# The first steps of an attention and feed-forward kernel, listed in another order

## The chip, the cores and the metric

The kernel runs on one NeuronCore of a Trainium2 chip. The metric is device time in microseconds (us) of one execution. An execution is also recorded by the hardware profiler; its span runs from the first to the last instruction of the program. The core's engines are PE (TensorE, matmuls and transposes into PSUM), DVE (VectorE), ACT (ScalarE), POOL (GpSimd) and SP (SyncE, which here only issues DMAs). Each takes its own instructions strictly in the order in which they were written.

## The reference

```python
# attention in chunks of 64 tokens: B=8, H=8, S=576, D=64
scores = scale * np.matmul(q_c, k_c.transpose(0, 1, 2, 4, 3))
scores = scores - np.max(scores, axis=-1, keepdims=True)
attn = np.exp(scores)
attn = attn / (np.sum(attn, axis=-1, keepdims=True) + 1e-09)
out = np.matmul(attn, v_c)
# the heads side by side give x of 4608 tokens x 512; then, with d_ff = 1024:
h = x @ w_in
e = np.exp(h - h_max)
sm = e / (np.sum(e, axis=-1, keepdims=True) + 1e-09)
solu = h * sm
ln = (solu - mu) / np.sqrt(var + 1e-06) * g_ln
return (ln @ w_out).astype(np.float32)
```

q, k and v are float32; w_in (512 x 1024) and w_out (1024 x 512) come as 64-bit floats, 4 MB each; g_ln has 1024 values.

## The kernel before

The 4608 tokens are 36 tiles of 128. A tile holds two chunks of 64 tokens with all 8 heads. Its way is: q and k (256 KB each) are loaded and turned, scores (PE), softmax (DVE, ACT, POOL or DVE), the weights turned, values (PE), the product with w_in into `ph` (PE), its softmax, sum and mean (DVE, ACT), z turned and split, the product with w_out (PE), and the store.

The products are made in pieces. A weight is split into a high and a low part (`wi_h`, `wi_l`, `wo_h`, `wo_l`), and the product of a tile with w_in is 24 matmuls of 128x128 by 128x512. Tiles 0 and 1 are an exception (FM = 2): they take the unsplit float32 weight `w_a` and the unsplit `x_f`, 8 matmuls that show as 16 in the profile.

The weights come in eight units: units 0 to 3 are 128 rows of w_in, 4 to 7 are 256 rows of w_out, 1 MB each as raw 64-bit words (`w_raw`). A unit passes through steps that other words of the list name: P loads it; c scales it (DVE or POOL by CL_DVE, then ACT); C shifts it and adds the low bits (two instructions of DVE); t makes the high part (ACT); D makes the low part (POOL for the halves in SUB_POOL, else DVE). With C done, `w_a` of the unit can be multiplied.

Up to tile 5 the order is written out by hand: START (lines 19 to 33) is a list of words, and lines 815 to 823 run them one after the other. A word as `N:2:1` is a step with its numbers; a word that stands several times continues its step each time from where it stopped. The words that matter here:

- n:i loads q and k of tile i in their natural layout (`nat`, or `nat_z` for tiles 2 and 3). N:i:0 and N:i:1 turn q and k of it: first four transposes on PE into a PSUM bank `po`, the second time the copy to `qT` or `kT` (DVE for those in NV_DVE, else ACT). There are two `po` banks, which N, T, z and F share.
- S:i scores; A:i maximum and subtraction (DVE), the second time the exponential (ACT); B:i sum and reciprocal (DVE), then the scaling of `e` (POOL for tiles in NORM_POOL, else DVE); T:i transposes `e` on PE and copies it to `attn_t`.
- v:i loads v; V:i values, then `x_f`, or `x_h` and `x_l`.
- M:i the product with w_in. M:0 goes on in four parts, one for each unit of w_in. X:i maximum, exponential; Y:i the product of `ph` and its exponential, which leaves z and frees `ph`; there is one `ph` buffer, so M:i+1 waits for Y:i. F is a third of a tile's product with w_out.
- W:x multiplies the identity by itself, with no use of the result. g loads g_ln, G turns it.

Behind START a loop makes tiles 5 to 35 in a fixed pattern, with tile i's product with w_in beside tile i-1's and i-2's product with w_out. SP issues nearly all loads into one queue, and a DMA's issue waits until the DMA eight places earlier has landed, or until a buffer is free.

Of the kernel before, what the change touches and what calls it, by code (L numbers as in the profile page):

```python
# [12 lines left out]
AF = mybir.ActivationFunctionType  # L13
# [3 lines left out]


START = """
W:41 W:42 n:0 n:1 N:0:1 N:0:0 N:0:0 N:0:1 N:1:0 n:2 S:0 N:2:1 N:1:0 A:0 A:0 P0 P1 P:2 N:1:1 B:0  # L20
P:1 c:0 c:2 N:1:1 W:43 c:0 N:2:0 S:1 W:44 W:45 W:46 N:2:1 N:2:0 n:3 c:2 C:0 A:1 A:1 C:0 B:0 c:1
B:1 S:2 T:0 N:3:0 T:0 W:47 g W:4 c:1 N:3:0 A:2 v:0 C:2 N:3:1 P:3 G P:4 t:0 V:0 N:3:1 n:4 C:1 B:1
G V:0 A:2 S:3 C:1 C:2 T:1 B:2 B:2 c:3 c:3 M:0 t:2 M:0 A:3 C:3 T:1 M:0 v:1 A:3 C:3 c:4 B:3 M:0
N:4:1 X:0 t:1 N:4:0 c:4 n:5 N:4:1 T:2 v:2 B:3 N:4:0 n:6 X:0 V:1 C:4 v:3 P:5 P:6 D:1:0 T:2 Y:0
S:4 T:3 C:4 N:5:0 V:1 A:4 t:3 A:4 P:7 T:3 D:1:1 M:1 t:4 N:5:1 D:3:1 B:4 D:2:1 N:5:0 D:0:1 D:2:0
D:0:0 Y:0 N:5:1 V:2 N:6:1 D:3:0 v:4 D:4:0 N:6:0 c:5 B:4 D:4:1 V:2 S:5 X:1 n:7 N:6:1 X:1 V:2 Y:1
z:0:1 N:6:0 V:3 z:0:1 c:5 R:0 A:5 z:0:0 C:5 A:5 z:0:0 V:3 C:5 M:2 z:0:1 T:4 c:6 B:5 z:0:0 V:3
Q:2 S:6 t:5 c:6 N:7:0 T:4 X:2 C:6 V:4 q:8 v:5 N:7:0 B:5 n:8 D:5:1 c:7 D:5:0 T:5 X:2 Y:2 C:6 T:5
F c:7 Y:2 t:6 C:7 N:7:1 C:7 N:7:1 D:6:1 D:6:0 M:3 F t:7 D:7:0 A:6 V:4 N:8:0 V:4 D:7:1 R:2 q:8
Y:1 N:8:0 V:5 S:7 X:3 Z:2 X:3 N:8:1 Y:3 A:7 N:8:1 A:6 q:8 q:8 F z:1:0 z:1:0 R:1 A:7 B:6 v:6  # L30
z:1:0 M:4 V:5 B:7 B:6 Y:3 U:6 o:0 B:7 Z:3 z:1:1 U:7 z:1:1 v:7 X:4 o:0 X:4 F z:1:1 Y:4 R:3 F K:9
F o:1 Y:4 o:1 V:5 R:4
"""


# [23 lines left out]
def chunk_attention_then_solu_ffn(  # L59
# [35 lines left out]
    MS = nc.gpsimd
# [29 lines left out]
    g_sb = const.tile([P, NFC], F32, name="g_sb")  # L125
    g_row = const.tile([NFC, P], F32, name="g_row")
# [10 lines left out]
    HALF = FF // 2  # L137
    raw_words = 2 if w_in.dtype != F32 else 1
# [28 lines left out]
    def unit_scale(x):  # L167
# [15 lines left out]
    def unit_round(x):  # L183
# [55 lines left out]
    QT, KT, V, QS, KS = {}, {}, {}, {}, {}  # L239
# [98 lines left out]
    def turn_natural(i, x):  # L338
# [25 lines left out]
    def attn(i, part):  # L364
        return (sx, sy)[i % 2 if order.on else part][:, :, part]
# [46 lines left out]
    def softmax_b(i):  # L412
# [15 lines left out]
    def attn_transpose(i):  # L428
# [148 lines left out]
    def solu_b(i):  # L577
# [162 lines left out]
    def load_first():  # L740
        load_pair(0)
        sync.dma_start(*early[0])
# [57 lines left out]
    def product():  # L800
# [150 lines left out]
```

## Time and profile before

| | |
|---|---|
| median of 3 runs | 476.33 us (475.26 to 476.84) |
| the profiled execution | 477.21 us, of which its span is 475.3 us |
| PE busy over the span | 461.9 us |
| DVE, ACT, POOL busy | 368.8, 249.9, 160.2 us |
| mean granted clock of PE | 0.993 |

The profiled execution took 0.88 us more than the median, and 1.9 us of it lie outside the span. A busy share of 97% on PE says that the span is nearly PE's work from end to end. In the 40 slices of the page only the first two and the last have PE below nine tenths; a slice is 11.9 us.

### The profile page before, as it was taken

What the parts mean: (1) busy time and instruction counts of PE and PEld (TensorE: products, weight loads), DVE (VectorE), ACT (ScalarE), POOL (GpSimd) and SP (SyncE); (2) the same over time, 40 slices, a digit from 0 to 9 for tenths busy, and PEclk for the clock granted to TensorE, in tenths of its full rate; (3) what the DMA queues carried; (4) which work ended last, traced back from release to release, by engine and by line L of the source; (5) the groups of instructions that cost most, each with busy time, mean ns of one, the idle gap of its engine ahead of it and who ended that gap; (6) DMA issues with size and microseconds to landing.
All of it is one profiled execution on the core that took longest, in us unless ns stands there. A gap on an engine that the chain in (4) does not pass through costs nothing.

```text
span 475.3 us, 10986 instructions
## 1 busy us (share of the span) xinstructions
PE 461.9 (97%) x4193; PEld 378.3 (80%) x4193; DVE 368.8 (78%) x511; ACT 249.9 (53%) x402; POOL 160.2 (34%) x305
## 2 busy tenths in 40 slices
PE   6699999999999999999999999999999999999996
PEld 5555888888888888888888888888888888888886
DVE  2799988798888787878788878797979797945430
ACT  2565985546464645454545555555555555554551
POOL 0338556350505050505050505032515141413300
PEclk9799999999999999999999999999999999999999
DMA  9999877878787877697348596948644435333211
GB/s 225 302 248 325 135 134 154 197 181 161 173 164 174 157 179 143 154 168 172 84 125 167 140 188 147 181 123 182 152 111 110 113 85 140 97 103 103 75 44 46
DMA packets 192996, 72.05 MB, mean 152 GB/s; under 512 B 177128, under 2 KB 177648, under 8 KB 192560
## 3 DMA queue, kind: packets, MB, share of 16 engines
q1 hardware_dynamic: 186528, 58.63, 55.4%
q0 software_dynamic: 6272, 12.60, 10.1%
q8 instruction: 33, 0.54, 0.5%
q14 instruction: 19, 0.16, 0.1%
q10 hardware_dynamic: 144, 0.13, 0.1%
HBM read 36.70 MB, written 9.44 MB: 97 GB/s over the span
## 4 chain that ended last, share of the span: by engine, by line
PE 94%; DMA 2%; SPq 2%; DVE 1%; issue 0%; DVEq 0%
PE po L50 44%; PE ph L50 42%; PE sx L50 5%; PE sy L50 4%; DMA nat_z<-in_q_dram 2%; SPq L50 2%; DVE w_a L50 0%; DVE z L50 0%; DVE h_nmax L50 0%; DVE qT L50 0%; DVE o_sb L50 0%; DVEq L50 0%
## 5 line engine op out<-in xcount | busy, mean ns | idle before, releaser
L50 PE MATMUL po<-wo_l,z_h 128*128 128x512 f32 x280 | 110.8, 396 | 0.0
L50 ACT ACTIVATE z<-ph,h_nmax 128x1024 f32<-128x1024 f32 x36 | 40.2, 1117 | 131.6 <-DVE h_nmax L50 131.5
L50 PE MATMUL po<-wo_h,z_h 128*128 128x512 f32 x280 | 109.3, 390 | 0.0
L50 PE MATMUL po<-wo_h,z_l 128*128 128x512 f32 x280 | 109.2, 390 | 0.0
L50 PE MATMUL ph<-wi_l,x_h 128*128 128x512 f32 x272 | 106.1, 390 | 0.0
L50 PE MATMUL ph<-wi_h,x_h 128*128 128x512 f32 x272 | 105.8, 389 | 0.0
L50 POOL TENSOR_TENSOR u<-ssq,eps 128x1 f32<-128x1 f32 x36 | 6.8, 189 | 225.6 <-ACT sq L50 225.6
L50 POOL DMA_DIRECT2D z_t<-z_b x136 | 67.7, 505 | 16.6 <-DVE z_b L50 10.5
L50 PE MATMUL ph<-wi_h,x_l 128*128 128x512 f32 x272 | 72.7, 389 | 0.0
L50 DVE TENSOR_REDUCE h_nmax<-ph 128x1 f32<-128x1024 f32 x36 | 44.0, 1221 | 34.8 <-PE ph L50 34.8
L50 PEld LDWEIGHTS po<-wo_l,z_h 128*128 128x128 f32 x280 | 52.5, 188 | 11.4
L50 PEld LDWEIGHTS po<-wo_h,z_l 128*128 128x128 f32 x280 | 52.6, 188 | 11.0
L50 PEld LDWEIGHTS po<-wo_h,z_h 128*128 128x128 f32 x280 | 52.6, 188 | 10.4
L50 PEld LDWEIGHTS ph<-wi_l,x_h 128*128 128x128 f32 x272 | 51.1, 188 | 10.7 <-issue 0.2
L50 PEld LDWEIGHTS ph<-wi_h,x_l 128*128 128x128 f32 x272 | 51.0, 188 | 10.6
L50 PEld LDWEIGHTS ph<-wi_h,x_h 128*128 128x128 f32 x272 | 51.1, 188 | 10.5
L50 DVE TENSOR_TENSOR z_l<-z_t,z_h 128x1024 fp32r<-128x1024 f32 (+1 forms) x35 | 40.7, 1164 | 21.0 <-ACT z_h L50 21.0
L50 DVE SCALAR_TENSOR_TENSOR z<-ph,z 128x1024 f32<-128x1024 f32 x36 | 44.0, 1224 | 13.8 <-ACT z L50 13.7
L50 ACT ACTIVATE z<-z,z_sum 128x1024 f32<-128x1024 f32 x34 | 39.2, 1153 | 21.4 <-DVE z L50 20.3
L50 DVE STREAM_TRANSPOSE z_b<-z 128x1024 f32<-128x1024 f32 x33 | 39.9, 1209 | 6.6 <-ACT z L50 3.1
L50 ACT ACTIVATE o_sb<-po,r 128x512 f32<-128x512 f32 (+1 forms) x36 | 24.3, 675 | 28.5 <-POOL r L50 20.8
L50 ACT ACTIVATE sq<-z 128x1024 bf16<-128x1024 f32 x36 | 37.6, 1043 | 2.5 <-POOL z L50 2.5
(88 smaller groups left out, 621.8 us busy)
## 6 DMA issues: line engine op xcount, KB each, us to landing
out_dram<-o_sb SPq DMA_DIRECT2D x35, 256.0 KB, 2.5
z_t<-z_b SPq DMA_DIRECT2D x128, 64.0 KB, 2.9
z_t<-z_b POOLq DMA_DIRECT2D x128, 64.0 KB, 2.8
q_st<-in_q_dram SPq DMA_DIRECT2D x96, 72.0 KB, 3.2
k_st<-in_k_dram SPq DMA_DIRECT2D x96, 72.0 KB, 2.9
v_sb<-in_v_dram SPq DMA_DIRECT2D x27, 256.0 KB, 4.3
w_raw<-in_moe_w_out_dram SPq DMA_DIRECT2D x4, 1024.0 KB, 7.2
attn_t<-a_b POOLq DMA_DIRECT2D x60, 64.0 KB, 3.6
```

The lines of the kernel that those rows point to most:

```text
L50: ins = make(*args, **kwargs)
```

## The change

START is written anew, the lists that assign steps to engines change with it, and g_ln is loaded by ACT's queue. Every step of the old list is in the new one (the loads of tiles 0 to 8, eight W, the eight units, the products of tiles 0 to 4). The first words:

```diff
-W:41 W:42 n:0 n:1 N:0:1 N:0:0 N:0:0 N:0:1 N:1:0 n:2 S:0 N:2:1 N:1:0 A:0 A:0 P0 P1 P:2 N:1:1 B:0
-P:1 c:0 c:2 N:1:1 W:43 c:0 N:2:0 S:1 W:44 W:45 W:46 N:2:1 N:2:0 n:3 c:2 C:0 A:1 A:1 C:0 B:0 c:1
...
+n:1 n:0 P0 P1 P:1 P:2 n:2 W:41 W:44 W:4 W:43 N:1:0 N:1:0 W:42 v:0 c:0 N:0:1 N:0:1 c:0 N:0:0
+N:0:0 N:1:1 S:0 A:0 A:0 n:3 B:0 N:1:1 C:0 W:45 c:2 S:1 B:0 T:0 T:0 A:1 C:0 c:2 N:2:0 N:2:0
...
-    NV_DVE = ((0, 1), (1, 0), (2, 1), (4, 0), (6, 1), (9, 1),)
-    MEAN_POOL = (3, 4,)
-    CL_DVE = (0, 3, 4,)
-    TV_DVE = (3,)
-    SUB_POOL = ((0, 0), (0, 1), (1, 0), (1, 1), (2, 0), (2, 1), (3, 0), (3, 1), (7, 0), (7, 1),)
-    NORM_POOL = (0, 1, 2, 3, 4, 5, 6, 7,)
+    NV_DVE = ((0, 0), (2, 0), (5, 1), (8, 0), (9, 1))
+    MEAN_POOL = (0, 3, 4)
+    CL_DVE = (2, 3, 7)
+    TV_DVE = ()
+    GM_ACT = ()
+    SUB_POOL = ((0, 0), (0, 1), (1, 0), (1, 1), (2, 0), (2, 1), (3, 0), (3, 1), (5, 0), (5, 1), (6, 0))
+    NORM_POOL = (0, 1, 5, 6)
     SH_POOL = ()
+    HALF_IN = (3,)
...
-            sync.dma_start(dst, src)
+            cut = HALF * raw_words if x in HALF_IN else 2 * HALF * raw_words
+            if x >= NCC:
+                sync.dma_start(dst, src)
+            else:
+                for n in range(0, 2 * HALF * raw_words, cut):
+                    sync.dma_start(dst[:, n:n + cut], src[:, n:n + cut])
...
-        sync.dma_start(g_row, g_ln.rearrange("(a p) -> a p", p=P))
+        nc.scalar.dma_start(g_row, g_ln.rearrange("(a p) -> a p", p=P))
```

GM_ACT is empty, so the lines that ask for it change nothing.

On SP, at the start of the program, the loads stood so before (`nat` is tile 0, then 1; `nat_z` tile 2, then 3; `w_raw` from w_in units 0, 2, 1 and 3):

```order
L50 DMA nat<-in_k_dram 128x8x64
L50 DMA nat_z<-in_q_dram 128x8x64
L50 DMA nat_z<-in_k_dram 128x8x64
L50 DMA w_raw<-in_moe_w_in_dram 128x1024 x2
L50 DMA w_raw<-in_moe_w_in_dram 128x2048 x2
L50 DMA nat_z<-in_q_dram 128x8x64
L50 DMA nat_z<-in_k_dram 128x8x64
L50 DMA g_row<-in_moe_g_ln_dram 8x128
L50 DMA v_sb<-in_v_dram 128x4x64
L50 DMA v_sb<-in_v_dram 64x4x64 x2
L50 DMA w_raw<-in_moe_w_in_dram 128x2048
```

and stand so now (`nat` is tile 1, then 0; the first three units are 0, 1 and 2, the last two halves are unit 3):

```order
L51 DMA nat<-in_k_dram 128x8x64
L51 DMA w_raw<-in_moe_w_in_dram 128x1024 x2
L51 DMA w_raw<-in_moe_w_in_dram 128x2048 x2
L51 DMA nat_z<-in_q_dram 128x8x64
L51 DMA nat_z<-in_k_dram 128x8x64
L51 DMA v_sb<-in_v_dram 128x4x64
L51 DMA v_sb<-in_v_dram 64x4x64 x2
L51 DMA nat_z<-in_q_dram 128x8x64
L51 DMA nat_z<-in_k_dram 128x8x64
L51 DMA w_raw<-in_moe_w_in_dram 128x1024 x2
```

Four loads of q and k precede the weights instead of six, tile 2 comes behind unit 2, and v of tile 0 ahead of tile 3; up to unit 3 the same loads are made, without g.

On ACT the first instructions before (`qT`, `kT` are copies out of PSUM, `e_99` the exponential of tile 0, `w_a` the scaling of a unit):

```order
L50 ACT_TABLE_LOAD
L50 COPY qT<-po 128x512
L50 ACTIVATE e_99<-e_99 128x4x128
L50 COPY kT<-po 128x512
L50 ACTIVATE w_a<-w_a 128x1024
L50 COPY qT<-po 128x512
```

and now:

```order
L761 DMA g_row<-in_moe_g_ln_dram 8x128
L51 ACT_TABLE_LOAD
L51 COPY qT<-po 128x512
L51 COPY kT<-po 128x512
L51 ACTIVATE w_a<-w_a 128x1024
L51 ACTIVATE e_99<-e_99 128x4x128
L51 COPY kT<-po 128x512
L51 COPY attn_t<-po 128x8x2x32
```

Unit 0's scaling now stands ahead of tile 0's exponential and of the copy of tile 1's k, which the scores of tile 1 read.

On PE, the product of tile 0 (`ph<-w_a,x_f`) and what stands before it was:

```order
L50 MATMUL sy<-attn_t,v_sb 64x64 x16
L50 MATMUL sx<-kT,qT 64x64 x16
L50 MATMUL po<-ident,e_100 128x128 x4
L50 MATMUL ph<-w_a,x_f 128x512 x8
L50 MATMUL po<-ident,nat 128x128 x8
```

and is now:

```order
L51 MATMUL sy_98<-attn_t_95,v_sb_138 64x64 x16
L51 MATMUL ph_119<-ident_79 128x128 x4
L51 MATMUL sx_97<-kT_226,qT_225 64x64 x16
L51 MATMUL ph_303<-w_a_142,x_f_264 128x512 x2
L51 MATMUL po_308<-ident_79,nat_z_184 128x128 x4
L51 MATMUL po_313<-ident_79,nat_z_184 128x128 x4
L51 MATMUL ph_303<-w_a_233,x_f_264 128x512 x2
L51 MATMUL po_334<-ident_79,nat_96 128x128 x4
L51 MATMUL ph_303<-w_a_195,x_f_264 128x512 x2
L51 MATMUL po_352<-ident_79,nat_96 128x128 x4
L51 MATMUL ph_303<-w_a_327,x_f_264 128x512 x2
```

The product was one block behind the turning of tile 3; now its four parts (units 0, 1, 2, 3) lie around the turning of tile 3 and of tile 4.

## Rows read from the trace of the kernel before

**Rows 1.** Parts 1 and 2 of the page: PE, and its clock in tenths.
```profile
PE 461.9 (97%) x4193; PEld 378.3 (80%) x4193; DVE 368.8 (78%) x511; ACT 249.9 (53%) x402; POOL 160.2 (34%) x305
...
PEclk9799999999999999999999999999999999999999
```

**Rows 2.** Windows: stretch, its length, busy time by engine (instructions), clock, DMA.
```profile
14.70:18.90 4.20, 1.26 (x36) 1.01 (x36) 3.57 (x5) 2.73 (x4) 2.13 (x3) 1.00 1.11 322
18.90:25.70 6.80, 5.68 (x82) 5.25 (x81) 5.47 (x10) 4.33 (x7) 2.45 (x2) 0.50 0.85 267
...
34.00:49.90 15.90, 14.62 (x212) 9.19 (x210) 15.52 (x19) 10.75 (x18) 13.91 (x10) 1.00 1.06 289
...
50.00:60.00 10.00, 10.00 (x108) 8.24 (x109) 9.61 (x14) 8.83 (x16) 5.02 (x5) 1.00 0.69 120
```

**Rows 3.** The chain that ended last: start, length, engine and line.
```profile
26.39 7.00 PE ph L50 x16
...
35.23 1.75 DVE w_a L50
...
38.27 7.10 PE ph L50 x16
...
49.88 5.67 PE ph L50 x24
```

**Rows 4.** Timeline of PE: start, length, operation, count, idle before and its releaser.
```profile
1.42 2.07 PE L50 MATMUL ph<-ident 128*128 128x128 f32 x8 [1.42 <-POOL e L393]
5.30 3.02 PE L50 MATMUL po<-ident,nat 128*128 128x128 f32 x12 [1.80 <-DMA nat<-in_k_dram]
...
10.04 0.63 PE L50 MATMUL po<-ident,nat_z 128*128 128x128 f32 x4 [0.93 <-DMA nat_z<-in_k_dram]
...
13.09 1.60 PE L50 MATMUL ph<-ident 128*128 128x128 f32 x12
17.64 0.69 PE L50 MATMUL sx<-kT,qT 64*64 64x64 f32 x32 [2.95 <-DVE e L50]
...
20.04 1.09 PE L50 MATMUL po<-ident,nat_z 128*128 128x128 f32 x4 [1.12 <-DMA nat_z<-in_q_dram]
...
23.82 1.13 PE L50 MATMUL sy<-attn_t,v_sb 64*64 64x64 f32 x32
...
35.14 0.69 PE L50 MATMUL sy<-attn_t,v_sb 64*64 64x64 f32 x32
```

**Rows 5.** Timeline of SP: its issues of DMAs, start and length.
```profile
8.77 0.89 SPq L50 DMA_DIRECT2D nat_z<-in_q_dram  x1
9.71 5.12 SPq L50 DMA_DIRECT2D nat_z<-in_k_dram  x1
14.87 2.76 SPq L50 DMA_DIRECT2D g_row<-in_moe_g_ln_dram  x1
```

**Rows 6.** Timeline of POOL, 16 to 20 us.
```profile
16.07 1.09 POOL L50 TENSOR_SCALAR w_a<-w_raw 128x1024 f32<-128x1024 f32 x1 [14.63 <-DMA w_raw<-in_moe_w_in_dram]
17.14 1.04 POOL L50 TENSOR_TENSOR e<-e,s_rinv 128x512 f32<-128x512 f32 x1
18.88 1.42 POOL L50 TENSOR_SCALAR w_a<-w_raw 128x1024 f32<-128x1024 f32 x1 [0.71 <-DMA w_raw<-in_moe_w_in_dram]
```

**Rows 7.** Timeline of DVE, steps of units and a copy.
```profile
13.59 0.69 DVE L50 TENSOR_SCALAR w_a<-w_raw 128x1024 f32<-128x1024 f32 x1 [1.27 <-DMA w_raw<-in_moe_w_in_dram]
14.20 0.68 DVE L50 COPY kT<-po 128x512 f32<-128x512 f32 x1
...
29.98 1.35 DVE L50 SCALAR_TENSOR_TENSOR w_a<-w_raw,w_a 128x1024 uint16<-128x1024 uint32 x1
```

**Rows 8.** Timeline of ACT, 10 to 15 us.
```profile
11.26 0.57 ACT L50 COPY kT<-po 128x512 f32<-128x512 f32 x1
...
14.32 1.06 ACT L50 ACTIVATE w_a<-w_a 128x1024 f32<-128x1024 f32 x1 [2.49 <-DVE w_a L50]
```

**Rows 9.** DMA issues within 20.1 to 20.6 us: unit 3, count, size, us to landing.
```profile
w_raw<-in_moe_w_in_dram SPq DMA_DIRECT2D x1, 1024.0 KB, 5.1
```

More of the change, by code (lines that the diff above doesn't have):

```diff
@@ L19 @@
 START = """
-W:41 W:42 n:0 n:1 N:0:1 N:0:0 N:0:0 N:0:1 N:1:0 n:2 S:0 N:2:1 N:1:0 A:0 A:0 P0 P1 P:2 N:1:1 B:0
-P:1 c:0 c:2 N:1:1 W:43 c:0 N:2:0 S:1 W:44 W:45 W:46 N:2:1 N:2:0 n:3 c:2 C:0 A:1 A:1 C:0 B:0 c:1
[L22 to L32, printed above, removed]
+n:1 n:0 P0 P1 P:1 P:2 n:2 W:41 W:44 W:4 W:43 N:1:0 N:1:0 W:42 v:0 c:0 N:0:1 N:0:1 c:0 N:0:0
+N:0:0 N:1:1 S:0 A:0 A:0 n:3 B:0 N:1:1 C:0 W:45 c:2 S:1 B:0 T:0 T:0 A:1 C:0 c:2 N:2:0 N:2:0
+c:1 c:1 A:1 C:2 N:2:1 V:0 W:47 N:2:1 g C:1 V:0 P:3 n:4 W:46 S:2 B:1 C:1 A:2 v:1 M:0
+N:3:0 N:3:1 A:2 C:2 n:5 N:3:0 P:5 N:3:1 B:1 c:3 M:0 c:3 N:4:0 N:4:0 M:0 B:2 P:4 t:0 C:3 D:0:1
+C:3 N:4:1 t:1 N:4:1 t:3 M:0 D:3:0 D:1:1 n:6 T:1 D:3:1 B:2 S:3 T:1 X:0 T:2 N:5:0 X:0 A:3 T:2
+V:1 V:1 S:4 N:5:0 N:5:1 D:1:0 A:3 Y:0 A:4 M:1 N:5:1 A:4 c:5 B:3 B:3 c:5 c:4 t:2 v:2 c:4
+N:6:1 P:6 T:3 C:5 N:6:1 n:7 B:4 B:4 C:5 V:2 X:1 G T:3 C:4 T:4 D:0:0 G X:1 S:5 Y:1
+T:4 V:2 Y:0 z:0:1 v:4 v:3 D:2:0 V:2 A:5 t:5 D:2:1 z:0:1 z:0:0 z:0:0 z:0:0 P:7 M:2 c:6 A:5 C:4
+B:5 N:6:0 R:0 t:4 D:4:0 v:5 z:0:1 X:2 c:6 V:3 C:6 N:6:0 S:6 V:3 n:8 V:3 X:2 N:7:0 N:7:1 N:7:0
+Y:2 Y:2 B:5 C:6 c:7 V:4 D:4:1 T:5 V:4 t:6 D:5:0 N:7:1 Y:1 V:4 D:6:0 D:6:1 Z:2 A:6 D:5:1 T:5
+M:3 c:7 z:1:0 C:7 v:6 F Q:2 R:2 X:3 C:7 X:3 F S:7 z:1:0 t:7 Y:3 D:7:0 A:6 D:7:1 Y:3
+z:1:0 A:7 R:1 q:8 V:5 V:5 F o:0 q:8 q:8 z:1:1 z:1:1 M:4 q:8 N:8:1 A:7 B:7 v:7 z:1:1 B:6
+B:6 R:3 F F X:4 Z:3 X:4 Y:4 Y:4 B:7 N:8:1 U:6 V:5 U:7 R:4 F o:1 o:1 o:0 K:9
+N:8:0 N:8:0
 """
@@ L209, in unit_high @@
                 g = g_sb[:, 2 * m + y:2 * m + y + 1]
-                act.activation(top[:, y], a[:, y], AF.Copy, scale=g)
+                act.activation(
+                    a[:, y] if x in GM_ACT else top[:, y], a[:, y], AF.Copy, scale=g
+                )
+            if x in GM_ACT:
+                act.copy(top, a)
         tops[x] = top
@@ L221, in unit_rest @@
             low = wo_l[:, 2 * m + y, :]
-            g = g_sb[:, 2 * m + y:2 * m + y + 1]
+            if x not in GM_ACT:
+                g = g_sb[:, 2 * m + y:2 * m + y + 1]
         of, part = a[:, y], top[:, y].bitcast(F32)
```

## The prediction

> **What bounds the kernel now.** I read the page first, then windows, then the chain of waits, then the engines' timelines of the first 50 us. The page gives PE 461.9 us of 475.3 [rows 1], so at most 13.4 us can be won, and some 3.5 of them are the last store. The windows say where: from 50 us on PE is busy 10.00 of 10.00, before that 14.62 of 15.90 and less [rows 2]. The chain agrees: from the product at 49.88, the first with a split weight (tile 2, M:2), it is PE alone [rows 3]. The reader is to see the idle times in PE's timeline: 1.42, 1.80, 0.93, 2.95 and 1.12 us [rows 4], with 1.28 between 34 and 49.9 [rows 2], together 9.5. A second loss is the clock. From 18.9 to 25.7 us it is granted at 0.50 (1.2 of 2.4 GHz), after a stretch in which PE worked 1.26 of 4.20 us [rows 2]; 5.68 us of work there would take half, so 2.8 are lost. It is low at the start too, where the page's row says full [rows 1]: twelve transposes take 3.02 us there, twelve like matmuls at 13.09 take 1.60 [rows 4]. So I measure the change by when M:2 begins, how much of PE's work is done by then, and what idle time comes behind it.
>
> **The loads.** One queue serves them in order. k of tile 0, the second load, is there at 5.30, k of tile 2, the sixth, at 10.04 [rows 4]: 1.19 us for each 256 KB. Units 0, 2, 1 are there at 13.59, 16.07 and 18.88 [rows 6, 7]. Now two loads fewer are ahead: units 0, 1, 2 at about 11.2, 13.7 and 16.5. Behind them come tile 2 (q 17.7, k 18.9), v of tile 0 (20.0), tile 3 (21.2, 22.4) and unit 3. Unit 3 landed at 20.08 + 5.1 = 25.2 [rows 9]; the same bytes are ahead of it, so 25.2 again. Its two halves win nothing, since the instruction that scales it reads both. g's issue held SP for 2.76 us, but 4 KB is no reason: the issue before it took 5.12 for what had taken 0.89 just before [rows 5], so SP was held up by what was queued. The load that follows inherits the hold; I count 0 for g (bounds 0 and 2.76 of SP's time, none of it on the path while transfers queue up).
>
> **PE up to tile 0's product.** Sixteen W matmuls at the start instead of eight last 3.5 to 4.1 us (twice 2.07 [rows 4]), to about 5.1. Tile 1 lands first; tile 0 is complete only at 5.30 + 2 x 1.19 = 7.7, and its scores end at 10.2. Then a new wait: the scores of tile 1 need the copy of k, which on ACT stands behind unit 0's scaling and tile 0's exponential. Unit 0 lands at 11.2, POOL takes 1.09 [rows 6], ACT 1.06 for the scaling and 0.57 each for the exponential and the copy [rows 8], both passes over 128x512: with a handoff, 14.6. PE has one W in between and is idle about 4.1 us. Tile 0's sum and scaling (0.9 on DVE, 1.04 on POOL [rows 6]) let its transposes start at 16.2, then q and k of tile 2 at 17.7 and 18.9, and values of tile 0 at 20.0, where before they began at 23.82 [rows 4]. From 10.2 to 17.7 PE works some 1.7 us, so I expect the low clock here as in the window from 14.70 [rows 2]. It came back 5.7 us after work resumed at 20.04 [rows 2, 4]; work now resumes at 17.7 to 19, so 23.4 to 24.7. Values then take 1.13 instead of 0.69 [rows 4], the eight W about 1.7, and the first part of M:0 starts at about 23.5 (before: 26.39 [rows 3]).
>
> **The end of tile 0's product.** A part is a quarter of 7.00 [rows 3], 1.75. The last part needs unit 3, and DVE is late with it, not the load. From unit 2's landing at 16.5 DVE has before it, in its order: 12 short passes of 0.69 [rows 7] (scalings, shifts, reductions, a copy), 8.3; two reciprocals, 0.4; four passes of 1.35 [rows 7] that finish units 0 to 3, 5.4. Together 14.1, so unit 3 is ready at 30.7. The parts before it end by 30 at the full clock (four parts and four turnings of 0.5 from 23.5, less the last part). M:0 ends at 30.7 + 1.75 = 32.5; before, 26.39 + 7.00 = 33.4. Won: 0.9.
>
> **From there to M:2.** M:1 waits for tile 0's z, which frees `ph`. Before, M:0's end to M:1's start took 38.27 - 33.39 = 4.88 us, in which DVE made a copy of 0.68 [rows 7] and a shift of 1.75 [rows 3] ahead of z. Now two short passes (1.4) stand there: 4.88 - 2.43 + 1.4 = 3.9. PE's seven groups take about as long. M:1 runs from 36.4 to 43.5 (7.10 [rows 3]); before to 45.37. Between M:1 and M:2 were eight groups in 49.88 - 45.37 = 4.51, 0.56 each; now seven and g's transpose: 4.2. M:2 starts at 47.7, 2.2 us earlier. But by then PE has made one turning and one values less and one transposing of e more: 0.6 of work is still to do. Net 1.6.
>
> **Behind M:2.** Before, eight matmuls of the product with w_out stood between M:2 and M:3; now that product begins only behind M:3. PE has seven groups, 3.9 us, while the way from M:2 over reduction, exponential and z takes about 4.2 with ACT's queue ahead of the exponential: 0.3 idle, and as much again before M:4. The engines' lists move: scalings of four tiles go from POOL to DVE (+2.7 us at 0.68), two copies and half a unit's low part leave DVE (-2.1), two copies come to ACT and one mean goes to POOL. DVE has 15.52 of 15.90 and 9.61 of 10.00 us full [rows 2], so its extra 0.6 can't hide there; bounds 0 and 1.4, and I take it as within the 0.6 just counted. Unit loads of w_out come later than before, behind tiles 4 and 5, but their first reader comes later by more; 0, and up to 1 if that is wrong. From M:5 on the loop is the same.
>
> The sum is 1.6 - 0.6 = 1.0 us off the profiled 477.21, so 476.2; that execution was 0.88 above the median, so the median goes from 476.33 to 475.3.
>
> **Rivals.** (1) *More of it stays.* Consecutive DVE passes often overlap by 0.05 or more, so the 17 passes may take 0.6 less, and PE then sets the end of M:0; if the idle 0.6 behind M:2 doesn't come either, 2.2 are won: 474.1. For it: the pass at 13.59 takes 0.69 and the next starts 0.61 behind its start [rows 7]. Against: passes of 1.35 slow down beside POOL, as the shift of 1.75 did [rows 3].
>
> (2) *The low clock stays through the first two parts of M:0.* The place is PE from 23.5. The new idle stretch, 10.2 to 17.7, is longer than the one that lowered the clock before, and work resumes with gaps for each load. If the clock is still low when the second part begins, near 27, both parts take 3.5 and the turning between them 1.7: 23.6 to 32.3, then two turnings and two parts at the full clock: 36.8, 4.3 later than 32.5. Result 3.3 slower: 479.6. Against it: from 19 on PE has no gap over 0.2.
>
> (3) *The clock comes back only after the first part.* Then 23.6 + 3.5, two turnings, 1.75 and so on end M:0 at 34.1, 1.6 late: 476.9. Row by row: the first twelve transposes stand 0.21 apart, the four at 10.04 stand 0.11 apart [rows 4], and between lie only 32 small score matmuls, so the clock did rise behind a run of mostly transposes. The Trainium skill (TensorE: Matmul & The Clock Gate, Part 4) says that transposes don't count as activity for the clock; by that rule PE's work would count from the values at 20.0 and this case would be it. The trace leans against that rule.
>
> (4) *Won early, lost later.* If ACT's queue holds tile 2's exponential by another 0.5 and tile 3's too, the whole 1.0 is idle before M:3 and M:4: 476.3. For it: ACT is 8.83 of 10.00 full [rows 2].
>
> **How the numbers follow.** Forecast 0.37 (its own range 474.5 to 476.3), rival (1) 0.24, (2) 0.20, (3) 0.08, (4) 0.11. A measurement of this kernel tells a difference from about 0.3%, 1.43 us: below 474.9 is faster, above 477.76 slower. Of the forecast's chance 0.08 lies below 474.9. Faster: 0.24 + 0.08 = 0.32. Slower: 0.20. Within: 0.48. The range runs from 473.3 (rival 1 with another 0.8 of idle time gone) to 478.2, between (3) and (2); it leaves out most of (2) and a little of (1).
>
> **What would show it.** Right: in PE's timeline a wait of 3 to 5 us before the second run of scores, released by ACT's `kT`; unit 0 read at about 11.2; the first part of M:0 at 23 to 24 and its end at 32 to 33; M:2 at 47 to 48.5; a short idle time before M:3. Wrong: the scores of tile 1 before 13; the last part of M:0 released by a load instead of DVE; the clock at 0.50 in 25 to 30 us; idle time on PE of over 1 us behind M:3.

## The result and the profile after

The changed kernel takes 479.59 us (median of 5, 478.87 to 480.86), the kernel before 476.33 beside it: 1.0068 times as long, 95% interval 1.0050 to 1.0087. It is slower by 0.7%, and the forecast of 475.3 with its range to 478.2 was wrong. Measured again on another chip (f4 below) it was 1.0083 [1.0050, 1.0116], with a median of 480.52 in five executions; a sixth, the profiled one, took 1184.61 us with PE slow from start to end and is left out.

The profiled executions stand 1.66 us apart (478.87 against 477.21), the medians 3.26: the profiles show half of the loss, and the changed kernel's is its fastest execution. First the page and the windows, as [rows 1, 2] show them for before:

```profile
PE 463.5 (97%) x4193; PEld 378.4 (79%) x4193; DVE 367.8 (77%) x512; ACT 249.4 (52%) x403; POOL 165.1 (35%) x304
...
14.70:18.90 4.20, 3.24 (x28) 2.31 (x24) 3.30 (x5) 1.80 (x3) 2.76 (x2) 0.50 1.04 189
18.90:25.70 6.80, 6.80 (x89) 4.81 (x88) 6.53 (x10) 3.58 (x7) 1.88 (x1) 0.88 1.05 248
34.00:49.90 15.90, 15.03 (x211) 9.71 (x212) 15.62 (x23) 11.96 (x20) 15.21 (x11) 1.00 0.96 266
50.00:60.00 10.00, 9.81 (x138) 7.88 (x137) 9.47 (x14) 8.32 (x15) 5.79 (x6) 1.00 0.86 218
```

The clock is low earlier, as forecast (0.50 in the first window), and back within the second. In the last window PE is no longer full: 9.81 of 10.00 us. Now PE's timeline (start, length, operation, count, idle time before and its releaser), to set beside [rows 3, 4]:

```profile
13.99 1.14 PE L51 MATMUL sx<-kT,qT 64*64 64x64 f32 x32 [3.11 <-ACT kT L51]
15.95 1.12 PE L51 MATMUL po<-ident,e 128*128 128x128 f32 x4 [0.82 <-POOL e L51]
...
22.27 1.98 PE L51 MATMUL ph<-w_a,x_f 128*128 128x512 f32 x4
24.09 1.04 PE L51 MATMUL po<-ident,nat_z 128*128 128x128 f32 x8
24.97 1.88 PE L51 MATMUL ph<-w_a,x_f 128*128 128x512 f32 x4
28.93 0.63 PE L51 MATMUL po<-ident,nat 128*128 128x128 f32 x4 [2.09 <-DMA nat<-in_q_dram]
29.40 1.88 PE L51 MATMUL ph<-w_a,x_f 128*128 128x512 f32 x4
31.12 0.60 PE L51 MATMUL po<-ident,nat 128*128 128x128 f32 x4
31.58 1.98 PE L51 MATMUL ph<-w_a,x_f 128*128 128x512 f32 x4
...
48.33 1.06 PE L51 MATMUL po<-ident,z 128*128 128x128 f32 x8 [0.79 <-DVE g_sb L51]
49.47 0.47 PE L51 MATMUL ph<-wi_l,x_h 128*128 128x512 f32 x1
...
58.64 0.63 PE L51 MATMUL po<-ident,e 128*128 128x128 f32 x4
59.41 0.50 PE L51 MATMUL ph<-wi_l,x_h 128*128 128x512 f32 x1
...
68.08 0.50 PE L51 MATMUL po<-wo_l,z_h 128*128 128x512 f32 x1 [0.37 <-POOL wo_l L51]
...
73.30 0.48 PE L51 MATMUL ph<-wi_l,x_h 128*128 128x512 f32 x1
```

The reader is to see M:0's four parts at 22.27, 24.97, 29.40 and 31.58: the first is 4 us earlier than before, the end (33.56) later by 0.2. M:2 begins at 49.47, M:3 at 59.41, M:4 at 73.30. M:2 and M:4 of the kernel before:

```profile
49.87 0.47 PE L50 MATMUL ph<-wi_l,x_h 128*128 128x512 f32 x1
...
72.16 0.48 PE L50 MATMUL ph<-wi_l,x_h 128*128 128x512 f32 x1
```

To compare two orders I count PE's useful work instruction by instruction, each kind at its spacing at full clock, and ask how much later the changed kernel has done the same amount. It is about 2 us earlier at 26 to 28 us of before, 0.3 later at M:0's end, 0.7 earlier during M:1, 0.2 later at M:2, 0.9 at 60.5, 1.6 at 70, and 1.78 from 97 on. The values at M:0's end and at M:2 hang on the spacing taken for the small score matmuls, by some 0.3 us either way. So what was won ahead of M:0 is lost before M:2, and behind M:2 about 1.6 more go. This second loss can be read without such a count. From M:2 to M:4 it takes 23.83 us, and in the kernel before 22.29. In the eight profiles with the changed order behind M:2 and a full clock there (the changed kernel, e1, e2, e4, e5, e7, e9 and e11), it is 23.80 to 23.86; in the three with the order of before there (the kernel before, e10 and f7), it is 22.29 to 22.31.

DVE on the two stretches where the lead goes (to set beside [rows 7]):

```profile
24.22 1.35 DVE L51 SCALAR_TENSOR_TENSOR w_a<-w_raw,w_a 128x1024 uint16<-128x1024 uint32 x1
27.61 0.69 DVE L51 TENSOR_SCALAR w_a<-w_raw 128x1024 f32<-128x1024 f32 x1 [2.04 <-DMA w_raw<-in_moe_w_in_dram]
...
30.15 1.37 DVE L51 SCALAR_TENSOR_TENSOR w_a<-w_raw,w_a 128x1024 uint16<-128x1024 uint32 x1
...
45.22 1.22 DVE L51 TENSOR_REDUCE h_nmax<-ph 128x1 f32<-128x1024 f32 x1
46.35 1.76 DVE L51 TENSOR_SCALAR w_a<-w_a 128x1024 uint32<-128x1024 uint32 x1
48.03 0.15 DVE L51 TENSOR_SCALAR g_sb<-po 128x8 f32<-128x8 f32 x1
48.11 1.21 DVE L51 SCALAR_TENSOR_TENSOR z<-ph,z 128x1024 f32<-128x1024 f32 x1
```

Before, M:1's maximum and its z stood so on DVE, behind M:1's end at 45.37:

```profile
46.01 1.21 DVE L50 TENSOR_REDUCE h_nmax<-ph 128x1 f32<-128x1024 f32 x1
...
48.49 1.22 DVE L50 SCALAR_TENSOR_TENSOR z<-ph,z 128x1024 f32<-128x1024 f32 x1
```

At 27.61 DVE had waited 2.04 us for unit 3: the load is late, not DVE. Its two halves took 8.3 us from issue to landing where the whole unit took 5.1 [rows 9]:

```profile
w_raw<-in_moe_w_in_dram SPq DMA_DIRECT2D x2, 512.0 KB, 8.3
```

### The profile page after: what moved, and what is told of

It reads as the page before. It is cut to its first block, busy times and chain, and to the rows that moved or that the text cites. A ratio compares the mean times of both kernels' runs of the same rounds, so it can differ in the third digit from the quotient of the medians.

```text
span 477.1 us, 10982 instructions
## 1 busy us (share of the span) xinstructions
PE 463.5 (97%) x4193; PEld 378.4 (79%) x4193; DVE 367.8 (77%) x512; ACT 249.4 (52%) x403; POOL 165.1 (35%) x304
## 4 chain that ended last, share of the span: by engine, by line
PE 89%; DVE 3%; DMA 3%; POOL 2%; ACT 1%; SPq 1%; issue 1%; DVEq 0%; POOLq 0%
PE po L51 43%; PE ph L51 38%; PE sx L51 4%; PE sy L51 3%; DMA nat<-in_q_dram 2%; DMA w_raw<-in_moe_w_in_dram 1%; SPq L51 1%; POOL w_a L51 1%; DVE w_a L51 1%; POOL wo_l L51 1%; ACT z L51 0%; DVE h_nmax L51 0%; DVE e L51 0%; DVE s_sum L51 0%; DVE z L51 0%
## 5 line engine op out<-in xcount | busy, mean ns | idle before, releaser
L51 POOL TENSOR_TENSOR u<-ssq,eps 128x1 f32<-128x1 f32 x36 | 7.9, 221 | 222.8 <-ACT sq L51 222.7
L51 POOL DMA_DIRECT2D z_t<-z_b x136 | 67.9, 506 | 18.9 <-DVE z_b L51 12.5
L51 PEld LDWEIGHTS ph<-wi_l,x_h 128*128 128x128 f32 x272 | 51.1, 188 | 11.2 <-DVE z L51 0.4
L51 ACT ACTIVATE z<-z,z_sum 128x1024 f32<-128x1024 f32 x33 | 38.1, 1153 | 22.3 <-DVE z L51 21.2
```

The lines of the kernel that those rows point to most:

```text
L51: ins = make(*args, **kwargs)
```

## The experiments

Theories: A, the halves make unit 3 late and M:0's end sets the time; C, DVE's list between M:0 and M:2 sets it; H, the loss lies behind M:2, where the first third of tile 0's second product was moved behind M:3. The diffs name words of START; all are against the changed kernel unless said. "Before" took 476.0 to 477.0 beside all of them. The intervals of e1, e2, e4, e5, e7 and e9 overlap the changed kernel's own, so their times can't be told from its time; these runs are read by their profiles, one each.

**e1, unit 3 whole.**
```
-    HALF_IN = (3,)
+    HALF_IN = ()
```


> Unit 3 of w_in in one DMA again (rows of 8192 B), all else as in the changed kernel. Theory A, the two halves with rows of 4096 B are slower: unit 3 lands at about 25.2 to 25.7 instead of 27.5, DVE scales it at about 25.6 instead of 27.6, q of tile 4 lands some 2 us earlier too, the 2.09 us wait ahead of M:0's third part falls to under 0.5, M:0 ends at 31.5 to 32 instead of 33.56, and the time falls by 1.3 to 2 us, to about 478. Theory B, the halves cost nothing and the queue is held by something else (SP's hold-ups, an instruction fetch): unit 3 still lands at 27 to 27.5 and the time stays within 0.5 us of the changed kernel's 479.6.


Measured 481.19, 1.0090 [1.0072, 1.0107]. DVE's scaling of unit 3 again begins at 27.61:
```profile
27.61 0.69 DVE L51 TENSOR_SCALAR w_a<-w_raw 128x1024 f32<-128x1024 f32 x1 [0.66 <-DMA w_raw<-in_moe_w_in_dram]
```
The halves aren't why it is late. That both begin at 27.61 is chance: in other profiles with the changed order DVE begins on unit 3 between 26.28 (f2, halves) and 28.50 (e5, halves), and at 26.49 in e4 (whole). In both kernels here tile 4's small rows follow unit 3 in the queue, where before a unit of w_out followed; that this is the reason wasn't tried.

**e2, M:0's third part ahead of tile 4's q; e4, both edits.**
```
-c:3 M:0 c:3 N:4:0 N:4:0 M:0 B:2
+c:3 M:0 c:3 M:0 N:4:0 N:4:0 B:2
```


> Only PE's order changes: M:0's third part stands ahead of the transposes of tile 4's q instead of behind them; unit 3 stays in halves. Theory A, unit 3 sets the end of M:0: the third part begins at about 26.9, the transposes wait for q of tile 4 until 28.9, the last part still begins at about 31.5 behind DVE, M:0 ends at 33.3 to 33.6 and the time changes by less than 0.3 us. Theory B, the order of PE (a ready part behind transposes that wait) sets it: M:0 ends at about 31.6 and the time falls by 1.5 to 2 us, to about 478.

> The first and second edit together: unit 3 in one DMA, and M:0's third part ahead of tile 4's q. By theory A (the landing of unit 3 sets the end) M:0 ends at 31.5 to 32 as with the first edit alone, time about 478, within 0.5 of that one. By theory B of the second edit (PE's order) the second edit adds 1 us or more to the first.


e2: 479.63, 1.0060 [1.0045, 1.0075]; the last part at 31.43, released by DVE, M:0's end 33.41. e4: 479.03, 1.0048 [1.0031, 1.0066]; M:0 ended at 32.42, 1.14 earlier. And M:2 began at 49.32 and 49.53. e4's PE:
```profile
48.40 1.06 PE L51 MATMUL po<-ident,z 128*128 128x128 f32 x8 [1.21 <-DVE g_sb L51]
49.53 0.47 PE L51 MATMUL ph<-wi_l,x_h 128*128 128x512 f32 x1
```
In e4 what M:0 won was lost again: M:1 began only 0.35 earlier (37.15), and PE then waited longer for DVE (1.21 instead of 0.79). It isn't always so. In f2 (below), whose edit lies behind M:2, unit 3 came early without an edit; M:0 ended at 32.22, and M:1 and M:2 began 1.34 and 0.81 earlier than in the changed kernel's profile:
```profile
36.16 7.11 PE L51 MATMUL ph<-w_a,x_f 128*128 128x512 f32 x16
...
48.66 0.47 PE L51 MATMUL ph<-wi_l,x_h 128*128 128x512 f32 x1 [0.23 <-DVE z L51]
```
So an M:0 that ends 1.1 to 1.3 us earlier brought M:2 0.81 forward in one profile and not at all in another. The halves of theory A are out; M:0's end has a part in M:2, but doesn't set it alone. In e4 and in f2 DVE, now earlier, waited 0.58 and 0.57 us for ACT's scaling of a unit of w_out.

**e7, one DVE pass less.**
```
-    NV_DVE = ((0, 0), (2, 0), (5, 1), (8, 0), (9, 1))
+    NV_DVE = ((0, 0), (2, 0), (8, 0), (9, 1))
```


> The changed kernel with the copy of tile 5's turned k on ACT instead of DVE (0.68 us of DVE at 38.60, in a stretch from 34 to 50 us in which DVE is busy 15.7 of 16 us and ACT 12.1). Theory C (DVE's work sets the pace there): all on DVE behind it comes 0.5 to 0.7 earlier, M:2 at 48.8 to 49.0 instead of 49.47, time lower by about 0.5. Rival, POOL and the landing of w_out's second unit (40.1) set it: M:2 at 49.3 to 49.5 and no change.


Measured 478.35, 1.0054 [1.0036, 1.0071], and M:2 where theory C put it, with M:0's end no earlier (33.70):
```profile
47.87 1.06 PE L51 MATMUL po<-ident,z 128*128 128x128 f32 x8 [0.19 <-DVE g_sb L51]
49.01 0.47 PE L51 MATMUL ph<-wi_l,x_h 128*128 128x512 f32 x1
```
M:2 itself shows little, since it moves as much between profiles whose lists are the same up to there (the changed kernel, e6, f2, f5). The way from M:1 to M:2 shows more, in us:

| profile | M:0 ends | M:1 begins | M:2 begins | M:1 to M:2 |
|---|---|---|---|---|
| before | 33.38 | 38.27 | 49.87 | 11.60 |
| changed kernel | 33.56 | 37.50 | 49.47 | 11.97 |
| e6, edit behind M:2 | 33.45 | 37.39 | 49.37 | 11.98 |
| f2, edit behind M:2 | 32.22 | 36.16 | 48.66 | 12.50 |
| f5, edit behind M:2 | 33.26 | 37.20 | 50.45 | 13.25 |
| e4 | 32.42 | 37.15 | 49.53 | 12.38 |
| e9 | 32.38 | 36.32 | 48.81 | 12.49 |
| e7 | 33.70 | 37.64 | 49.01 | 11.37 |
| f3, with e7's edit | 33.23 | 37.17 | 48.57 | 11.40 |

With the pass off DVE it is 11.4 in both e7 and f3; in every profile of the changed order that has the pass it is 11.97 or more. (e8 and e12 also have e7's edit, but further edits on the same way, and took 12.25 and 14.94.) So DVE's list lies on the way from M:1 to M:2, as theory C said. e7 has the lowest median with the changed list, but its interval overlaps e4's and the changed kernel's: that it is faster isn't shown.

**e5, g turned early; e9, POOL's work taken away.**
```
-N:3:1 B:1 c:3 ... X:1 G T:3 ... D:0:0 G X:1
+N:3:1 B:1 G G c:3 ... X:1 T:3 ... D:0:0 X:1
```
```
+    nc.gpsimd.memset(wi_l[:, 2:4, :].bitcast(U32), 0)
...
+        if x in (2, 3):
+            return
```


> The changed kernel with the turn of g (one transpose, one scaling to g_sb) moved ahead of unit 3's scaling, where DVE is idle for 2.04 us; before it stood behind M:1's maximum on DVE. Theory C, what counts is DVE's list between M:0 and M:2: the 0.79 us wait of the transposes of z for g_sb goes, M:2 begins at 48.6 to 48.9 instead of 49.47 and the time falls by 0.5 to 0.8. Theory D, the loss comes from loads and the clock ahead of M:0: the time stays within 0.3 of 479.6.

> The changed kernel without the low part of units 2 and 3 of w_in: their four subtractions (on POOL, 1.3 to 1.7 us each, four of them from 41.8 to 49.3) are left out and that half of wi_l is set to zero at the start, so this part of the computation is missing. Theory E, passes of DVE and of POOL over SBUF hold each other up: the shifts on DVE at 40.79 (1.61 us) and 46.35 (1.76 us) are back at 0.69 or nearly, z of tile 0 on POOL takes 1.4 instead of 2.55, M:2 begins at 47.5 to 48.5 instead of 49.47, the time falls by 1 to 2 us. Rival F, only the count of DVE's passes sets the pace: M:2 stays at 49.0 to 49.5 and the time within 0.4 of the changed kernel's.


e5: 481.01 (477.94 to 481.76), 1.0085 [1.0059, 1.0110]; M:2 at 52.34 in the profile, which is of its slowest execution. Its DVE, its POOL and its PE:
```profile
41.73 2.93 DVE L51 TENSOR_SCALAR w_a<-w_a 128x1024 uint32<-128x1024 uint32 x1
...
46.15 2.44 DVE L51 SCALAR_TENSOR_TENSOR w_a<-w_raw,w_a 128x1024 uint16<-128x1024 uint32 x1
```
```profile
44.21 1.44 POOL L51 TENSOR_SCALAR z<-z,z_sum 128x1024 f32<-128x1024 f32 x1
45.73 3.94 POOL L51 TENSOR_TENSOR wi_l<-w_a,wi_h 128x512 fp32r<-128x512 f32 x2
```
```profile
51.45 0.66 PE L51 MATMUL po<-ident,z 128*128 128x128 f32 x4 [2.67 <-ACT attn_t L51]
```
A shift of 0.69 took 2.93 and a pass of 1.33 took 2.44, beside POOL's; POOL's two subtractions took 3.94 (three took 3.75 in the changed kernel). So M:1's maximum came at 48.45 instead of 45.22, and PE's wait for ACT's copy stands behind it, since that copy stands behind M:1's exponential in ACT's list.

In the changed kernel's profile it is POOL's z that is long, 2.56, beside a DVE pass of 1.33 at 44.01. The Trainium skill (SBUF — State Buffer, section "SBUF: two separate sides") says that DVE and GpSimd share a pair of ports under an exclusive lock: where a DVE instruction needs that pair (in its two-port mode, or with two SBUF inputs beside a GpSimd instruction that reads SBUF), whichever starts first keeps it for its whole instruction and the other stands. The rows agree as far as they go: which of the two is lengthened changes from profile to profile, often by about the other's length; in which mode a pass ran they don't show.

In e9 (478.78, 1.0043 [1.0026, 1.0059]) z took 1.43, as expected, and one shift 1.02, but two other passes still met POOL (1.58 and 1.75), and M:2 came at 48.81, 0.66 earlier with M:0's end 1.2 earlier. From M:1 to M:2 it took 12.49, as long as f2 with all of POOL's work in place (12.50). So e9 shows no gain on that way from taking POOL's work off, and what the collisions cost in all stays open.

**e6, POOL's order; e8, five edits together.**
```
-D:6:0 D:6:1 Z:2 A:6 D:5:1 T:5
+D:5:1 D:6:1 Z:2 A:6 D:6:0 T:5
```


> The changed kernel with two words changed about, so that POOL makes the low part of unit 5's second half ahead of unit 6's first half. Theory C (order behind M:1): the wait of 0.37 us for wo_l at 68.08 goes, tile 0's second third of product runs on without a break, M:4 begins some 0.4 to 0.6 earlier (72.8 instead of 73.30), the time falls by about 0.5. Theory D: within 0.2 of 479.6, since the wait is replaced by one for unit 6 or for M:4's x.


Measured 483.25, 1.0146 [1.0115, 1.0177]. The wait at 68 went, and longer ones for DVE's low parts of unit 7 took its place, so M:4 began at 74.36, later by 1.06 (theory C had 72.8, theory D the same time):
```profile
71.67 0.50 PE L51 MATMUL po<-wo_l,z_h 128*128 128x512 f32 x1 [0.75 <-DVE wo_l L51]
...
73.20 0.50 PE L51 MATMUL po<-wo_l,z_h 128*128 128x512 f32 x1 [0.57 <-DVE wo_l L51]
```
e8 joins e4, e5, e6 and e7; expected:


> Five edits of the changed kernel together: unit 3 in one DMA, M:0's third part ahead of tile 4's q, g turned early, unit 5's second half ahead of unit 6's first on POOL, tile 5's k copied by ACT. By theory C the gains add: 479.0 (first two) less 0.7, 0.5 and 0.5, about 477.3, M:2 at 48.2 to 48.6, M:4 at 71.5 to 72. If it is as low as the kernel before (476.3 to 476.8), the loss of the change is explained by these places; if it stays at 479, theory C is wrong.


It took 481.31, 1.0112 [1.0094, 1.0129], with M:2 at 51.41 and 25.01 us from M:2 to M:4. The second is e6's loss (24.99 there); the late M:2 was not followed up. The run doesn't decide on theory C.

**e3, the engine lists of before with the new order.**


> The order list of the changed kernel with the engine lists of the kernel before (which engine does the copies of turned q and k, the clamps, the subtractions, the scalings by the row sum, the means). Theory A, of the 2 us that the changed kernel is behind, about 1.5 come behind M:1 from lists that put units 5 and 6 of w_out on POOL and the scalings of tiles 2 to 4 on DVE: the time falls by about 1.5, to 478, and the product of tile 2 begins at 48.5 or earlier and the wait for POOL at 68 is gone. Theory B, order and lists hang together, or the loss behind M:1 has another cause: the time is the same or longer (479.5 to 482), because unit 0's clamp goes to DVE, which is busy at 10 to 16 us, and the copies of tile 0 change engine.


501.88, 1.0518 [1.0494, 1.0542]; waits for POOL and DVE of 1.7 to 3.4 us at six places. Theory A is out. Theory B has the direction, but not the size (up to 482): the engine lists of before don't fit the new order.

**e11, the clock held up; e12, POOL's mean on ACT too (with e7's edit).**
```
-W:45 c:2 S:1
+W:45 W:48 W:49 W:50 W:51 ... c:2 S:1
```
```
-    MEAN_POOL = (0, 3, 4)
+    MEAN_POOL = (3, 4)
```


> The changed kernel with twelve more idle products (24 matmuls of 128x128) in the 3.11 us wait ahead of tile 1's scores. Theory G for the changed kernel: the clock stays at full speed, M:0's first part begins at 20 to 21 instead of 22.27, but its later parts wait for unit 3 (27.5) and q of tile 4 (28.8) as before, M:0 ends at 33.3 to 33.6 and the time stays within 0.4 of 479.6. Rival (the clock is the cause): M:0 ends 1.5 to 2 earlier and the time falls by 1.5 to 3.

> The changed kernel with two passes moved to ACT, which is idle for 1.3 and 2.2 us between 39 and 46: the copy of tile 5's k (from DVE) and the mean of tile 0 (from POOL, 2.55 us at 43.65). Theory E: M:2 begins at 48.2 to 48.8, time 0.5 lower than with the first alone (478.35 on its chip), about 477.8. Rival F (DVE's count): the same as the first alone, M:2 at 49.0.


e11: 482.24, 1.0123 [1.0102, 1.0144]. The clock was full to 28 us and M:0 began at 22.45, no earlier, so the low clock hadn't held it up. Then the clock fell behind the wait for tile 4's q, and the third part ran at half of it:
```profile
29.35 0.67 PE L51 MATMUL po<-ident,nat 128*128 128x128 f32 x4 [2.32 <-DMA nat<-in_q_dram]
29.82 3.58 PE L51 MATMUL ph<-w_a,x_f 128*128 128x512 f32 x4
```
e12: 483.99, 1.0157 [1.0123, 1.0191]. On ACT the mean stood behind other passes and PE waited for it; the clock fell behind that wait (windows of e12, as above):
```profile
50.01 1.97 PE L51 MATMUL po<-ident,z 128*128 128x128 f32 x8 [3.28 <-ACT z L51]
...
50.00:54.00 4.00, 3.99 (x14) 3.51 (x15) 2.47 (x4) 3.73 (x7) 0.00 (x0) 0.50 0.76 170
```

**e10, before again; f1, before with the third moved.**
```
-... C:6 T:5 F c:7 ... D:6:0 M:3 F t:7
+... C:6 T:5 c:7 ... D:6:0 M:3 F F t:7
```


> The kernel before, profiled once more. Its eleven executions beside the last runs had a mean granted clock between 0.991 and 1.000 and times between 475.4 and 477.2, the longest with one of the lowest clocks. Theory G: the stretch at half clock that its first profile shows from 18.9 to 25.8 is missing or shorter in most of its executions, and then M:2 begins 1 to 1.5 earlier than 49.87; the changed kernel had no execution over 0.993. Rival: the clock changes nothing behind M:0, since DVE sets that; M:2 at 49.5 to 49.9 whatever the clock.

> The kernel before, with one word of its list moved: the first third of tile 0's second product (8 matmuls, 1.9 us) stands behind M:3 as in the changed kernel, not ahead of it. Theory H, this third is what PE does while DVE and ACT free the bank for M:3: M:3 can't begin before z of tile 2 is done (60.2 in the first profile), PE waits some 1.5 us ahead of it, M:3 to M:4 grows by about 1.7 (M:4 at 73.5 to 74 instead of 72.16), and the time rises by 1.3 to 1.9, to about 478.2, with no other change. Rival: the wait is made good again before M:6, time within 0.4 of before.


e10 (one time, 476.77): the low clock was shorter (granted 0.72 in 20 to 21 us, 0.50 in 21 to 23, 0.57 in 23 to 24), M:0 began 0.8 earlier than in the first profile, and M:2 came at 49.49, 0.38 earlier, where theory G had 1 to 1.5. M:4 came at 71.79, so M:2 to M:4 took 22.30 as in the first profile. PE of before and then of f1 ahead of M:3:
```profile
57.76 0.66 PE L50 MATMUL po<-ident,e 128*128 128x128 f32 x4
58.17 0.48 PE L50 MATMUL po<-wo_l,z_h 128*128 128x512 f32 x1
...
60.10 0.60 PE L50 MATMUL po<-ident,nat 128*128 128x128 f32 x4
60.45 0.48 PE L50 MATMUL ph<-wi_l,x_h 128*128 128x512 f32 x1
```
```profile
57.60 0.60 PE L50 MATMUL po<-ident,nat 128*128 128x128 f32 x4
59.60 0.50 PE L50 MATMUL ph<-wi_l,x_h 128*128 128x512 f32 x1 [1.40 <-DVE z L50]
...
73.14 0.48 PE L50 MATMUL ph<-wi_l,x_h 128*128 128x512 f32 x1
```
With M:2 at 49.18, M:2 to M:4 is 23.96: 1.67 more, by a word that changes only PE's order, and the lag at equal work keeps the 1.67 to the end. The time is 477.72, 1.0026 [1.0008, 1.0045], +1.2 us with 0.4 to 2.1. Theory H holds in the kernel before.

**f2 and f5, the third back ahead of M:3; f3, f2 with e4 and e7.**
```
-Y:2 Y:2 B:5 C:6 c:7 V:4 D:4:1 T:5 ... T:5 M:3 ... v:6 F Q:2
+D:4:1 Y:2 Y:2 B:5 C:6 c:7 V:4 T:5 ... T:5 F M:3 ... v:6 Q:2
```
f5 also draws both words N:7:1 behind that F.


> The changed kernel with the first third of tile 0's product ahead of M:3 as in the kernel before, and the low part of unit 4's second half (DVE) drawn ahead of z of tile 2, which that third needs. Theory H1, only the place of the third counts: the hidden wait ahead of M:3 goes and the time falls by 0.5 to 0.7. Theory H2, the lateness of w_out's units counts (unit 5's second half made by POOL until 68.0, unit 7's by DVE until 71.7): the third no longer waits ahead of M:3, but the next thirds wait longer at 68 (0.8 to 1.2 instead of 0.37) and at 71, and the time stays within 0.3.

> The edit f2 once more, with the turn of tile 7's k moved behind that third: in f2 the third had to wait 3.67 us for a bank that this k held until ACT copied it. Now the third has a bank at once. Theory H1 (the place of the third alone): no wait ahead of M:3, M:2 to M:4 about 23.2 instead of 23.8, time 0.5 to 0.7 below the changed kernel. Theory H2 (w_out's late units bind anyway): M:3 at about 61.2 without a wait, then 0.5 to 1 us of wait for unit 5's second half (POOL, 68.0) or unit 7 (DVE, 71.7), M:2 to M:4 at 23.6 to 24 and the time within 0.4.


486.0 (1.0204 [1.0175, 1.0232]) and 485.63 (1.0187 [1.0171, 1.0202]), where H1 and H2 both expected 479 to 480. f2, then f5:
```profile
62.12 0.79 PE L51 MATMUL po<-wo_l,z_h 128*128 128x512 f32 x1 [3.67 <-ACT kT L51]
```
```profile
64.95 0.87 PE L51 MATMUL po<-ident,nat 128*128 128x128 f32 x4 [3.06 <-ACT attn_t L51]
```
Each `po` tile holds a bank until ACT copies it, and the third holds one of the two through M:3. In the changed order tile 7's k and tile 5's e lie in them, and their copies stand on ACT behind the mean, x_h and wo_h. So these two moves of the third's words couldn't bring it back, and H1 against H2 stays open. f3, at 485.53 (1.0191 [1.0164, 1.0218]), ran into the same wait (3.60).


> The edits that lowered the time or should: unit 3 in one DMA, M:0's third part ahead of tile 4's q, tile 5's k copied by ACT, the first third ahead of M:3. By theory H1 about 477.3 (479.6 less 0.6, 1.2 and 0.6, not all adding), by H2 about 477.9. Both expect it at or above the kernel before.

**f4, the changed kernel again**, is told of in the section on the result.


> The changed kernel once more, as the reference on the same chip and for a second profile. Expected: 479.3 to 480.0, M:2 at 49.3 to 50, M:2 to M:4 23.8 us as in all kernels with its list (22.3 in both profiles of the kernel before), and a clock of 0.989 or 0.993.

**f7, before with the clock held up.**
```
-B:1 S:2 T:0 N:3:0 T:0
+B:1 W:48 W:49 W:50 W:51 W:52 ... S:2 T:0 W:53 W:54 W:55 N:3:0 T:0
```


> The kernel before with thirteen more idle products (26 matmuls of 128x128) in its waits of 2.95 us ahead of tile 2's scores and 1.12 us ahead of tile 3's transposes. In the runs so far its executions at a mean clock of 1.000 took 474.5 to 476.7, those at 0.993 476.9 to 477.8. If the half clock from 18.9 to 25.8 costs it that, the clock is now full there in all executions, M:0 begins at 23 to 24.5 and M:2 at 48.5 to 49.2 instead of 49.87, and the median is 475.0 to 475.8, below both kernels. Rival: DVE (unit 3's last pass ends at 31.3) sets the end of M:0 whatever the clock, as in the changed kernel; M:2 at 49.3 to 49.9 and the median within 0.4 of before, or above it where the added products delay tile 2's scores.


477.03, 1.0010 [0.9998, 1.0021]. The clock was full, but the added products lasted 4.5 us and not 3 (one row of 6.07 where 1.60 stood), so tile 2's scores came at 20.98 and M:0 at 27.26. M:2 came at 50.25. No gain, and no clean test. No kernel tried beats the kernel before.

## Why the prediction was wrong

**The loads.** Right up to tile 3: unit 0 was read at 10.77 (forecast 11.2), q and k of tile 2 landed at 16.97 and 18.16 (17.7 and 18.9), those of tile 3 at 20.93 and 22.49 (21.2 and 22.4). Wrong for unit 3: "the same bytes are ahead of it, so 25.2 again"; it landed at 27.51, and why stays open. That its halves win nothing was right, and by e1 and e4 they cost nothing that can be seen either. g by ACT's queue was not tried by itself.

**PE up to M:0.** Right, with smaller sizes: the wait ahead of tile 1's scores by ACT's `kT` was 3.11 (forecast 4.1), T:0 at 15.95 (16.2), the clock low and back at 20.6 (23.4 to 24.7), M:0's first part at 22.27 (23.5). Rival (3) rested on the rule of the Trainium skill (TensorE: Matmul & The Clock Gate, Part 4) that transposes don't count as activity for the clock. By it PE's work would count from the values at 19.31 on only, and the clock was back at 20.6, when their row ended, and not behind M:0's first part. The trace leans against the rule, no more.

**The end of tile 0's product.** "DVE is late with it, not the load" was wrong. DVE stood 2.04 us for unit 3 and PE 2.09 for tile 4's q behind it, so M:0 ended at 33.56 instead of 32.5. What this cost further on isn't settled: with M:0's end 1.1 to 1.3 earlier, M:2 came no earlier in e4 and 0.81 earlier in f2.

**From there to M:2** is the first step that failed, "Net 1.6": at M:2 the changed kernel was some 0.2 behind instead. 1.1 of the missing 1.8 were gone at M:0's end. From there to M:1 the step held: 3.94 us (forecast 3.9). The other 0.7 went between M:1's end and M:2, which the prediction took as seven groups of PE and g's transpose, 4.2 us; it took 4.86, where before it took 4.50. PE's groups don't set that pace, DVE's list does: M:1's maximum begins 0.61 behind M:1's end, much as before (0.64), but from it to z it took 2.89 us against 2.48, since a shift of 0.69 took 1.76 beside POOL, and g's scaling stands there too. e7 and f3 show that a pass taken off DVE makes the way from M:1 to M:2 0.6 shorter.

**Behind M:2** is the second step that failed, a term mis-sized: 0.6 was counted for the third that now stands behind M:3, and 0 for w_out's later units; 1.54 was measured from M:2 to M:4, and about 1.6 by the count of work. f1 puts 1.67 on that move in the kernel before. In the changed kernel the hole ahead of M:3 is partly filled, and the rest shows as the wait of 0.37 for POOL's `wo_l` and the starts around it. How the loss divides there between the third's place and the late units stays open.

Together 1.1, 0.7 and some 0.9 are the 2.7 us between the forecast for the profiled execution (476.2) and the measured one (478.87).

**The rivals.** 479.6 was rival (2)'s time, but that is chance: its mechanism didn't happen, since the clock was back before M:0 began. It did happen in e11, for one part, and cost 1.7 us there. Rival (4), won early and lost later, is what came about, at a higher price and through DVE and the missing third rather than ACT.

**Not explained:** the 1.6 us by which the medians differ beyond the profiles. The changed kernel's executions run from 478.30 to 482.15 us in f4, those of the kernel before beside them from 474.47 to 477.79. In f4 the two at a mean clock of 0.993 took 478.30 and 479.11, the three at 0.986 to 0.989 took 480.52 to 482.15; in the first five there is no such order. Profiles show two ways in which an execution can lose more: in e3, e11, e12, f2, f3 and f5 the clock fell once more behind a new wait, and in e1 PE waited 0.58 us at 92.22 for the DMA `attn_t<-a_b`, which it doesn't do in the changed kernel's profile. That the kernel's other executions lose so is possible, and not shown; none of those was profiled.

## What to carry to other kernels

A lead on the bottleneck engine can end at the next place where another engine's list sets the pace; before pricing an edit, ask at each later start (here M:2 and M:3) which engine releases it, and whether that engine's work moved too. Work that fills the bottleneck while a single buffer is being freed is worth nearly its full length where it stands: in the kernel before, eight matmuls moved behind M:3 cost 1.67 of their 1.9 us. And a step moved back needs the buffers that it had, not only its place in the order.

## What the runs showed of the hardware

- Passes of DVE and POOL over SBUF were longer where they ran beside each other: DVE's 0.69 became 1.62, 1.76 (the changed kernel) or 2.93 (e5), 1.33 became 2.44 (e5), POOL's 1.43 became 2.56 (the changed kernel). Which of the two was lengthened changed from profile to profile.
- PE's clock was at 0.50 behind waits of 2.32 (e11), 3.11 (the changed kernel at 13.99) and 3.28 us (e12), and at 1.00 behind waits of 2.09 (the changed kernel at 28.93), 2.67 (e5 at 51.45) and 2.83 us (e3 at 39.65): the length of the wait alone doesn't tell. Held full to 28 us (e11) and over the early waits (f7), it brought no gain; both runs also added work, so neither is a clean test.
- Unit 3, 1 MB in rows of 8 KB, took 5.1 us from issue to landing in the kernel before, with a unit of w_out next in the queue (6.4 in e10). With tile 4's 256-byte rows next, DVE began on it between 26.28 and 28.50 us, whole or in halves; the two halves took 8.3 us.
